# Opening of a four-layer attention kernel: gate loads, input parts and identity products moved

## The chip, the cores and the metric

The kernel runs on one core of a Trainium2 chip. The metric is the device time of one execution in microseconds (us). Five engines run side by side, each through its own list of instructions in order: PE (matrix products; loading of its weights is shown as PEld), DVE (vector), ACT (activations), POOL (GpSimd) and SP, which here only issues DMAs.

## The reference

The input `x` is 2048 tokens of 640 numbers, in float32. Four residual layers follow, A, B, A, B, each on a layer norm of `x`, with 32 heads of 20 numbers. Layers of one kind share their weights.

```python
# A: linear attention
phi = lambda t: jnp.where(t > 0, t + 1, jnp.exp(t)) + 1e-6
pq, pk = phi(q), phi(k)
kv = jnp.einsum("bhsd,bhse->bhde", pk, v)
z  = jnp.einsum("bhsd->bhd", pk)
o  = einsum(pq, kv) / (einsum(pq, z) + 1e-6)          # then @ wo
# B: four segments of 512 tokens; causal softmax inside a segment, a running memory between them
g = _sigmoid(beta).reshape(1, H, 1, 1)
o = g * a_mem + (1.0 - g) * a_dot                     # then @ wo
```

`beta` (32 numbers) is the input that the gate loads below fetch.

## The kernel before

**Tiling.** Tokens go in 4 segments of 512, each in 4 tiles of 128. Products run in fp16 with float32 sums: an operand is kept as an upper part and a lower part (what the upper leaves over), and each product is made of three, upper by upper, upper by lower and lower by upper. For one output bank of 320 columns that is 5 chunks times 3 products (`proj_n`).

**The opening** is the first A layer (`opening`). Besides its own work it prepares all eight weight matrices. `w_prep` does that for one matrix in steps: five loads into a `stage` buffer, five DVE maxima (`wmx`), one maximum over them (`wm1`), a PE transpose of that column (L252), a DVE maximum of the turned row (`wm2`, L254), a PE product with ones that spreads it over the partitions (L258), three DVE instructions to a scale (`inv`, `scl`), then per chunk an ACT write of the upper part (L269) and a DVE write of the lower part (L270), and a store of the result to memory. Between the steps stand `pause`s, which let other work be recorded first. `w_Ak` is prepared at the very start, `A_q` in segment 0, `A_v` and `A_o` in segment 1, then `B_v`, `B_q`, and in segment 3 `B_k` and `B_o`.

In each segment `g_first` makes keys and queries (`phi_a`: ACT exponential and relu, one DVE combination), splits the keys into `pk` (ACT L556 upper, DVE L543 lower), and sums key by input products in `memory` (L580, 12 products a bank, DVE L602 adds them to `G`). Each tile is normalized (`moments`: DVE statistics, a POOL power for `rs`, DVE `nb`; then `normed` on ACT), turned by PE (`turn`: transposes L329, ACT upper L333, DVE lower L334) and also kept unturned as `xs` (`parts`: ACT L487, POOL L488), the weights of the `memory` products. After segment 3, `merge` folds the sums and the weights of `v` and `o` into one matrix: DVE makes `ge` (L661) from `G` and `rz`, ACT and DVE split it into `xT` (L663, L664), PE makes `kt` (L682) and then `wm` (L712, L718). `p_read` prepares query tiles for the next step; its row sum is the DVE reduction L757 into `rca`.

`gates` loads `beta` twice: as `gate` (one DMA) and as `cg` (four DMAs of eight numbers each, into a tile that DVE has filled first, L207). ACT takes exponentials of both (L211, L212), DVE adds one (L213, L214). It is called in `last`, in segment 3.

**What sets the order.** Generators are woven together; the order in which they record is PE's order (PE is scheduled by hand). On the other engines a scheduler places each instruction as early as it thinks it can run. `issue_after(i)` keeps what is recorded in its block behind instruction `i` on the engine of `i`. `busy(n)` records `n` products of the identity with itself, whose result nobody reads; each stands as two entries in the trace.

Of the kernel before, what the change touches and what calls it, by code (L numbers as in the profile page):

```python
# [21 lines left out]
P = 128  # L22
# [6 lines left out]
HN = 320  # L29
# [100 lines left out]
def pause(n):  # L130
    for _ in range(n):
        yield 0.0
# [12 lines left out]
class Kernel:  # L145
# [53 lines left out]
    def gates(self):  # L199


        nc, cp = self.nc, self.cp
        beta = self.A["B_beta"]
        g = cp.tile([P, H], F32, name="gate")
        nc.sync.dma_start(g, bass.AP(tensor=beta.tensor, offset=beta.offset, ap=[[0, P], [1, H]]))
        self.cg = cp.tile([P, NG], F32, name="cg")
        nc.vector.memset(self.cg, -1e4)  # L207
        for h4 in range(4):
            nc.sync.dma_start(self.cg[32 * h4 + DH:32 * h4 + DH + 1],
                              bass.AP(tensor=beta.tensor, offset=beta.offset + h4, ap=[[0, 1], [4, NG]]))  # L210
        nc.scalar.activation(g, g, AF.Exp, scale=-1.0)  # L211
        nc.scalar.activation(self.cg, self.cg, AF.Exp)  # L212
        nc.vector.tensor_scalar(g, g, 1.0, None, op0=OP.add)  # L213
        nc.vector.tensor_scalar(self.cg, self.cg, 1.0, 2.0 ** 100, op0=OP.add, op1=OP.min)  # L214
        self.ginv = g
# [15 lines left out]
    def w_prep(self, key, stage, w, wait=0, behind=None):  # L231


        nc, cp = self.nc, self.cp
        st = stage.tile([P, C, D], F32, tag="stage", name="stage", bufs=2)
        src = self.w_src(key).rearrange("(c p) n -> p c n", p=P)
        mx = cp.tile([P, C], F32, name="wmx", tag="wmx", bufs=2)
        for c in range(C):
            nc.sync.dma_start(st[:, c], src[:, c])
        yield from pause(wait)  # L240
        with self.tc.issue_after(behind.ins) if behind else nullcontext():
            for c in range(C):
# [5 lines left out]
        nc.vector.tensor_reduce(m1, mx, axis=AX.X, op=OP.max)  # L248
        yield 0.0
        yield from pause(wait - 4 if key == ("B", "o") else wait)  # L250
        pt = self.bank()
        nc.tensor.transpose(pt[:1, :P], m1, self.ident)  # L252
        m2 = cp.tile([1, 1], F32, name="wm2", tag="wm2", bufs=2)
        self.last = nc.vector.tensor_reduce(m2, pt[:1, :P], axis=AX.X, op=OP.max)  # L254
        yield 100.0
        yield from pause(wait + 2 if key == ("A", "v") else wait)
        pb = self.bank()
        nc.tensor.matmul(pb[:, :1], self.ones, m2, start=True, stop=True)  # L258
        inv = cp.tile([P, 1], F32, name="inv_%s%s" % key)
        scl = cp.tile([P, 1], F32, name="scl_%s%s" % key)  # L260
        nc.vector.tensor_scalar(inv.bitcast(I32), pb[:, :1].bitcast(I32), 0x7F800000, None,
                                op0=OP.bitwise_and)
        nc.vector.tensor_scalar(inv, inv, 2.0 ** -14, 2.0 ** -114, op0=OP.mult, op1=OP.max)
        self.last = nc.vector.reciprocal(scl, inv)
        self.inv[key], self.scl[key] = inv, scl
        yield 100.0
        for cols in (slice(0, HN), slice(HN, D)) if key == ("A", "k") else (slice(0, D),):
            for c in range(C):
                nc.scalar.activation(w[:, c, 0, cols], st[:, c, cols], AF.Copy, scale=scl)  # L269
                self.last = nc.vector.scalar_tensor_tensor(w[:, c, 1, cols], st[:, c, cols], scl, w[:, c, 0, cols],  # L270
                                                           op0=OP.mult, op1=OP.subtract)
# [50 lines left out]
    def turn(self, src, dst, i):  # L322

        nc = self.nc
        for c0, c1 in ((0, 3), (3, 5)):
            pt = self.bank()
            n = c1 - c0
            for c in range(c0, c1):
                nc.tensor.transpose(pt[:, (c - c0) * P:(c - c0 + 1) * P], src[:, c * P:(c + 1) * P],  # L329
                                    self.ident)  # L330
            v = pt[:, :n * P].rearrange("p (c t) -> p c t", c=n)
            hi = dst[:, c0:c1, 0, i * P:(i + 1) * P]
            nc.scalar.activation(hi, v, AF.Copy)  # L333
            self.lower = nc.vector.tensor_tensor(dst[:, c0:c1, 1, i * P:(i + 1) * P], v, hi, op=OP.subtract)  # L334
            yield n * 110.0

# [3 lines left out]
        self.nc.sync.dma_start(x, src[r:r + P])  # L340
        return x

    def moments(self, x):
# [8 lines left out]
        self.taken = nc.vector.tensor_scalar(rs, mv[:, 1:2], 1e-5, None, op0=OP.add)  # L352
        self.power = nc.gpsimd.tensor_tensor(rs, rs, self.mhalf, op=OP.pow)
        nb = sb.tile([P, 1], F32, tag="nb", name="nb", bufs=4)
        self.last = nc.vector.tensor_scalar(nb, mv[:, 0:1], rs, -1.0, op0=OP.mult, op1=OP.mult)
        return x, nb, rs

    def gather(self, x, mv):
# [36 lines left out]
                yield 9 * SEG * COL  # L395
        return p

    def proj_n(self, xT, w, i, n, p=None, cs=range(C)):

        nc = self.nc  # L400
        if p is None:
            p = self.bank()[:, :HN]
        k = 3 * cs[0]
        for c in cs:
            for a, b in ((0, 0), (0, 1), (1, 0)):
                nc.tensor.matmul(p, xT[:, c, a, i * P:(i + 1) * P], w[:, c, b, n * HN:(n + 1) * HN],  # L406
                                 start=k == 0, stop=k == 3 * C - 1)
                k += 1
        return p

    COST_N = 15 * HN * COL
# [122 lines left out]
    def g_first(self, s, box, w, L, behind=None):  # L534
# [12 lines left out]
        def keys(i):  # L547
# [4 lines left out]
            nc.gpsimd.memset(pk[i][:, 1, HN:HN + 1], 0.0)  # L552
            for n in range(2):
                z, c = slice(n * HN, (n + 1) * HN), slice(n * (HN + 1), n * (HN + 1) + HN)
                e = self.phi_a(self.proj_n(xT, w("k"), i, n), self.inv["A", "k"])
                nc.scalar.activation(pk[i][:, 0, c], e, AF.Copy, scale=self.k_scl)  # L556
                if L["early"] and s == 0 and i < NT - 1:
                    late.append((pk[i][:, 1, c], e, pk[i][:, 0, c]))
# [67 lines left out]
    def merge(self, L, wv, wo, memory, fill):  # L626
# [24 lines left out]
        for n in range(2):  # L651
# [4 lines left out]
            for c in range(C):  # L656
# [7 lines left out]
                nc.vector.tensor_tensor(t[:, c, 1, :HN], e, t[:, c, 0, :HN], op=OP.subtract)  # L664
        L["zb"] = zb
        L["pre"] = [self.p_load(L, 0, i) for i in range(3)]
        for _ in memory:
# [79 lines left out]
    def p_read(self, L, s, i, o, pq=None):  # L747
# [9 lines left out]
        nc.vector.tensor_reduce(rc, q3, axis=AX.X, op=OP.add)  # L757
# [377 lines left out]
    def opening(self, src, stage, L, box):  # L1135
# [15 lines left out]
        def w(n):  # L1151
            for _ in a(n):
                pass
            return self.w["A", n]

        def late():
            self.setup_late(stage)
            yield 0.0

        def last():  # L1160
            self.scales("B")
            with self.tc.issue_after(self.keyed.ins):
                self.gates()
            yield 0.0

        self.lower = self.keyed = self.first = None
        cur = [None, self.x_t(), self.xs_t(0)]
        k = a("k")
# [17 lines left out]
        self.key_scale()  # L1186
        m = [m]
        with self.tc.issue_after(self.last.ins):
# [15 lines left out]
        o = others()  # L1204
        self.ones_columns()
# [160 lines left out]
```

## Time and profile before

| | |
|---|---|
| time, median of 3 executions | 1705.25 us (1703.31 to 1706.91) |
| the profiled execution | 1704.55 us, of which its span is 1702.8 us |
| PE busy | 1637.9 us, 96% of the span, 13788 products |
| DVE busy | 1272.3 us, 75% |
| ACT busy | 994.2 us, 58% |
| POOL busy | 505.9 us, 30% |
| mean granted PE clock | 0.992 of full |
| first A layer | the first 262 us, of which the change touches most |

A row of the timeline gives the start in us, the duration, the engine, the line, the operation, output and inputs by name, the shape and the count; in brackets stands the idle time of the engine ahead of it and what ended that. A row of the windows gives a stretch, its length, busy time (number of instructions), the granted PE clock as a share of full speed, and the use of DMA.

### The profile page before, as it was taken

To read this page: it belongs to the slowest core of one execution; us is meant where nothing else is said; L and a number is where in the kernel's file an instruction comes from. 1 tells how busy PE (TensorE), PEld (TensorE's weight loads), DVE (VectorE), ACT (ScalarE), POOL (GpSimd) and SP (SyncE) were. 2 spreads that over 40 slices of the span, in tenths; PEclk is the share of its full clock that TensorE was granted. 3 is DMA by queue.
4 is the path that set the end of the run, shared out by engine and by line. 5 is a ranking of instruction groups with operands and counts; after the bars stand their busy time and mean duration, and the time that the engine had idled before them with its cause. 6 is when DMAs were issued, how large, how long until landed. Compare 5 with 4: busy or idle time off the path is not lost.

```text
span 1702.8 us, 37843 instructions
## 1 busy us (share of the span) xinstructions
PE 1637.9 (96%) x13788; PEld 1018.6 (60%) x13788; DVE 1272.3 (75%) x4015; ACT 994.2 (58%) x1888; POOL 505.9 (30%) x1046
## 2 busy tenths in 40 slices
PE   7999979999999999999999999999999999999998
PEld 5767757554465556556566777765546545645555
DVE  7888887487887788759874465847888978878773
ACT  6666533347756746667776454333675676666673
POOL 3442222013223322333452210310322332233452
PEclk9999989999999999999999999999999999999999
DMA  6424654421322331353211303423232323323432
GB/s 218 151 75 169 223 203 152 136 98 59 111 79 69 115 118 56 128 183 95 72 56 39 117 32 125 178 94 123 70 110 89 114 83 110 102 86 111 140 103 95
DMA packets 110372, 191.00 MB, mean 112 GB/s; under 512 B 14172, under 2 KB 69596, under 8 KB 107624
## 3 DMA queue, kind: packets, MB, share of 16 engines
q1 hardware_dynamic: 97704, 142.68, 25.9%
q0 software_dynamic: 3264, 24.91, 4.1%
q10 hardware_dynamic: 9216, 20.98, 3.2%
q8 instruction: 109, 1.79, 0.4%
q14 instruction: 79, 0.65, 0.1%
HBM read 109.32 MB, written 78.64 MB: 110 GB/s over the span
## 4 chain that ended last, share of the span: by engine, by line
PE 66%; DVE 17%; ACT 9%; issue 3%; DMA 3%; POOL 2%; SPq 0%; ACTq 0%; POOLq 0%; DVEq 0%
PE ps L406 25%; PE ps L391 13%; PE ps L1061 8%; PE ps L580 4%; PE ps L1034 4%; ACT pe L1038 3%; PE ps L993 3%; PE ps L329 3%; DVE ps L999 3%; PE ps L457 2%; PE ps L1074 1%; DVE e L421 1%; DVE wmx L243 1%; DVE split L270 1%; DVE xT L334 1%
## 5 line engine op out<-in xcount | busy, mean ns | idle before, releaser
L999 DVE CUSTOM_DVE_ANT_0 ps<-ps,maskw 128x512 f32<-128x512 f32 (+3 forms) x1024 | 472.0, 518 | 28.7 <-PE ps L993 25.9
L1038 ACT ACTIVATE pe<-ps,lsc 128x512 f32<-128x512 f32 x640 | 395.4, 696 | 63.0 <-PE ps L1034 59.8
L406 PEld LDWEIGHTS <-xT 128*128 128x128 f16 x2880 | 282.2, 99 | 115.0 <-issue 6.2
L1045 POOL TENSOR_SCALAR_AFFINE_SELECT pe<-pe 128x256 f32<-128x256 f32 (+1 forms) x640 | 233.4, 372 | 350.5 <-ACT pe L1038 342.7
L406 PEld LDWEIGHTS <-oT 128*128 128x128 f16 x1920 | 184.5, 98 | 84.7 <-issue 8.3
L1061 PE MATMUL ps<-pe,v 128*32 128x512 f32 (+3 forms) x2048 | 161.6, 436 | 8.8 <-DVE oT L334 1.9
L406 PE MATMUL ps<-wm,oT 128*128 128x320 f16 x960 | 141.3, 299 | 3.8 <-DVE rs L352 2.6
L406 PE MATMUL ps<-w_Bo,oT 128*128 128x320 f16 x960 | 141.5, 299 | 3.2 <-ACT oT L333 2.0
L406 PE MATMUL ps<-w_Ak,xT 128*128 128x320 f16 x960 | 140.6, 303 | 3.1 <-DVE xT L334 1.0
L406 PE MATMUL ps<-w_Bv,xT 128*128 128x320 f16 x960 | 142.3, 303 | 0.2
L391 PE MATMUL ps<-xT,w_Bq 128*128 128x512 f16 x600 | 140.9, 379 | 1.3 <-ACT pe L1038 0.8
L999 DVE DVE_READ_ACCUMULATOR2_ANT mg<- 128x1 f32 x1024 | 142.1, 139 | 0.1
L580 PE MATMUL ps<-pk,xs 128*128 128x321 f16 (+1 forms) x960 | 140.7, 304 | 1.1 <-DVE pk L543 0.7
L391 PE MATMUL ps<-xT,w_Bk 128*128 128x512 f16 x600 | 138.5, 379 | 1.2 <-ACT pe L1038 1.2
L406 PE MATMUL ps<-w_Aq,xT 128*128 128x320 f16 x960 | 137.6, 299 | 0.1
L993 PE MATMUL ps<-ks,qs 60*128 60x512 f16 (+3 forms) x1024 | 123.5, 297 | 7.6 <-ACT pe L1038 3.5
L580 PEld LDWEIGHTS <-xs 128*128 128x128 f16 x960 | 93.9, 99 | 41.0 <-issue 1.6
L421 DVE SCALAR_TENSOR_TENSOR e<-e,r 128x320 f32<-128x320 f32 x128 | 69.6, 544 | 53.6 <-ACT r L420 53.0
L1034 PE MATMUL ps<-qs,ks 62*128 62x512 f16 (+3 forms) x1024 | 105.6, 300 | 2.1 <-ACT pe L1038 1.1
L1061 PEld LDWEIGHTS ps<-pe,v 128*32 128x32 f32 x2048 | 65.4, 109 | 68.7 <-issue 40.9
L831 DVE SCALAR_TENSOR_TENSOR nat<-ps,nat 128x512 f16<-128x512 f32 x80 | 55.2, 690 | 62.6 <-ACT nat L830 62.3
L391 PEld LDWEIGHTS <-w_Bk 128*128 128x128 f16 x600 | 57.1, 98 | 66.5 <-issue 6.4
(202 smaller groups left out, 2359.6 us busy)
## 6 DMA issues: line engine op xcount, KB each, us to landing
x<-xn ACTq DMA_DIRECT2D x48, 320.0 KB
qs<-qd SPq DMA_DIRECT2D x128, 120.0 KB
ks<-kd SPq DMA_DIRECT2D x128, 120.0 KB
xo<-x SPq DMA_DIRECT2D x48, 320.0 KB
pqi<-pqd SPq DMA_DIRECT2D x32, 320.0 KB
qd<-nat SPq DMA_DIRECT2D x40, 256.0 KB
kd<-nat SPq DMA_DIRECT2D x40, 256.0 KB
x<-in_A_x SPq DMA_DIRECT2D x16, 320.0 KB
```

What stands on the lines that cost most here:

```text
L329: nc.tensor.transpose(pt[:, (c - c0) * P:(c - c0 + 1) * P], src[:, c * P:(c + 1) * P], self.ident)
L391: nc.tensor.matmul(p, w[:, c, a, t * P:(t + 1) * P], xT[:, c, b, :], start=k == 0, stop=k == 3 * C - 1)
L406: nc.tensor.matmul(p, xT[:, c, a, i * P:(i + 1) * P], w[:, c, b, n * HN:(n + 1) * HN], start=k == 0, stop=k == 3 * C - 1)
L421: nc.vector.scalar_tensor_tensor(e, e, 1.0, r, op0=OP.min, op1=OP.add)
L580: nc.tensor.matmul(p, xs[:, i, a, c * P:(c + 1) * P], pk[i][:, b, cols], start=i == 0 and a == b, stop=i == NT - 1 and a == 1)
L831: nc.vector.scalar_tensor_tensor(nat[:, 1], p, QK_SHIFT, nat[:, 0], op0=OP.mult, op1=OP.subtract)
L993: nc.tensor.matmul(bs[par][:, a:a + n], qs[r, p, i * P:(i + 1) * P], ks[r, p, :n], start=True, stop=True)
L999: nc.vector.tensor_tensor_reduce(bs[par][:, a:a + n], bs[par][:, a:a + n], self.maskw[:, SEG - n:], 1.0, NEG, OP.add, OP.max, G["mg"][:, p ...
L1034: nc.tensor.matmul(b[:, a:a + n], ks[r, p, j * P:(j + 1) * P], qs[r, p, j * P:], start=True, stop=True)
L1038: nc.scalar.activation(e, b, AF.Exp, scale=self.lsc)
L1045: nc.gpsimd.affine_select(d, d, pattern=pat, compare_op=OP.is_ge, fill=0.0, base=0, channel_multiplier=-1)
L1061: nc.tensor.matmul(G["pv"][32 * h4:32 * h4 + 32, j * P:], v[j][:, h * E1:h * E1 + 32], G.pop((p, par, j)), start=j == 0, stop=j == 2, skip ...
```

## The change

1. `gates` is split by a `yield`. Its loads are recorded in segment 1 (`late`, at the step `next(gates)`), the exponentials and additions in segment 3 as before, now behind the ACT instruction that last wrote an upper part of a turned tile (`self.upper`).
2. In segment 0 `parts` of a tile is recorded after the turn of the next tile and behind its ACT write and the last power on POOL, instead of all four after the last turn.
3. `busy`: 11 instead of 5 after the first turn, the 3 before `A_k`'s ones product instead of behind it, 5 behind it, and 4 after the second key product. With `cold`, the first key bank takes lower by upper ahead of upper by lower.
4. `moments` can stop ahead of `nb`; for tile 1 `nb` (`shift`) comes later among the lower parts of `w_Ak`.
5. `A_v` pauses 8 steps instead of 2 ahead of its ones product.
6. `p_read`'s row sum goes behind the last lower part that `merge` wrote (`L["parted"]`).

```diff
+        yield 0.0
+        with self.tc.issue_after(self.upper.ins):
+            nc.scalar.activation(g, g, AF.Exp, scale=-1.0)
+            nc.scalar.activation(self.cg, self.cg, AF.Exp)
...
-        yield from pause(wait + 2 if key == ("A", "v") else wait)
+        yield from pause(wait + 8 if key == ("A", "v") else wait)
...
+            for a, b in ((0, 0), (1, 0), (0, 1)) if cold else ((0, 0), (0, 1), (1, 0)):
...
+                if cold and k == 2 and n == 0:
+                    self.busy(4)
...
+        with self.tc.issue_after(L["parted"].ins):
+            nc.vector.tensor_reduce(rc, q3, axis=AX.X, op=OP.add)
...
         def late():
             self.setup_late(stage)
+            next(gates)
             yield 0.0
...
             with self.tc.issue_after(self.keyed.ins):
-                self.gates()
+                next(gates, None)
...
-        self.busy(5)
+        self.busy(11)
         with self.tc.high_priority():
-            for _ in range(4):
+            for _ in range(3):
                 next(k)
             self.busy(3)
+            next(k)
+            self.busy(5)
             with self.tc.issue_after(self.last.ins):
-                m = self.moments(x[1])
+                m = self.moments(x[1], False)
             with self.tc.issue_after(self.taken.ins):
-                w("k")
+                for _ in range(5):
+                    next(k)
+            with self.tc.issue_after(self.last.ins):
+                m = self.shift(*m)
+            w("k")
...
-            with self.tc.issue_after((self.keyed or top).ins):
-                for i in range(NT):
-                    self.parts(xh[i], cur[2], i)
+                for j in range(i - 1, NT if i == NT - 1 else i):
+                    with self.tc.issue_after(self.upper.ins), self.tc.issue_after(top.ins):
+                        self.parts(xh[j], cur[2], j)
```

How instructions stand on the engines, before and in the change (in these rows a line of the changed file is 2 to 7 higher for the same instruction). First DVE at the end of segment 3, where `wm_2790` and `wm_2815` are the turned maximum of `B_o`. Before:

```order
L570 TENSOR_SCALAR e<-e 128x320
L602 TENSOR_TENSOR v_81<-ps,v_81 128x321
L659 TENSOR_SCALAR eps<-v_81,k_scl 128x1
L214 TENSOR_SCALAR cg<-cg 128x8
L602 TENSOR_TENSOR v_82<-ps,v_82 128x321
L254 TENSOR_REDUCE wm_2790<-ps 1x1
```

In the change, the same place:

```order
L577 TENSOR_SCALAR e<-e 128x320
L609 TENSOR_TENSOR v_81<-ps,v_81 128x321
L666 TENSOR_SCALAR eps<-v_81,k_scl 128x1
L609 TENSOR_TENSOR v_82<-ps,v_82 128x321
L256 TENSOR_REDUCE wm_2815<-ps 1x1
```

The addition on `cg` has moved up beside that on `gate`, seven rows earlier. The filling of `cg` now stands fourth on DVE in the whole program, its four DMAs stand on SP right behind that of `gate` and ahead of the store of `w_Ak`, and both exponentials stand on ACT in segment 2, behind a turned tile.

Then PE at the start of the program, from the end of the first turn to the first key products. Before:

```order
L320 MATMUL ps<-ident 128x128 x5
L252 MATMUL ps<-ident,wm_163 1x128
L258 MATMUL ps<-wm_167,ones 128x1
L320 MATMUL ps<-ident 128x128 x3
L406 LDWEIGHTS xT
L406 MATMUL ps<-w_Ak,xT 128x320
```

In the change:

```order
L322 MATMUL ps<-ident 128x128 x11
L254 MATMUL ps<-ident,wm_169 1x128
L322 MATMUL ps<-ident 128x128 x3
L260 MATMUL ps<-wm_173,ones 128x1
L322 MATMUL ps<-ident 128x128 x5
L411 LDWEIGHTS xT
L411 MATMUL ps<-w_Ak,xT 128x320
L411 LDWEIGHTS xT
L411 MATMUL ps<-w_Ak,xT 128x320
L322 MATMUL ps<-ident 128x128 x4
```

Fifteen identity products are new, and three have gone ahead of the ones product. On DVE, `nb` of tile 1 stood behind the first of the ten lower parts of `w_Ak` and stands behind the sixth; on ACT and POOL the `xs` work has left the place ahead of the second key bank's exponential and ahead of the powers.

Last, PE between segments 1 and 2, where `wm_1574`/`wm_1633` is the column of `A_o` and `wm_1606`/`wm_1651` its turned maximum. Before:

```order
L580 LDWEIGHTS xs
L580 MATMUL ps<-pk,xs 128x320
L258 MATMUL ps<-wm_1606,ones 128x1
L406 LDWEIGHTS xT
L406 MATMUL ps<-w_Ak,xT 128x320
```

In the change:

```order
L587 LDWEIGHTS xs
L587 MATMUL ps<-pk,xs 128x320
L254 MATMUL ps<-ident,wm_1633 1x128
L260 MATMUL ps<-wm_1651,ones 128x1
L411 LDWEIGHTS xT
L411 MATMUL ps<-w_Ak,xT 128x320
```

The transpose of `A_o` stood 24 memory products ahead of its ones product and now stands right before it. `A_v`'s ones product stood ahead of the first memory product of segment 1 and now stands behind the 36th. On DVE the scale of `A_v` and its first lower parts go behind three of the copies L602, and the casts of the constants (L187, L188) behind the lower parts of `A_o`.

More of the change, by code (lines that the diff above doesn't have):

```diff
@@ L332, in turn @@
             hi = dst[:, c0:c1, 0, i * P:(i + 1) * P]
-            nc.scalar.activation(hi, v, AF.Copy)
+            self.upper = nc.scalar.activation(hi, v, AF.Copy)
             self.lower = nc.vector.tensor_tensor(dst[:, c0:c1, 1, i * P:(i + 1) * P], v, hi, op=OP.subtract)
@@ L341, in load_x, with moments @@
         return x
-    def moments(self, x):
+    def moments(self, x, whole=True):
         nc, sb = self.nc, self.sb
@@ L353, in moments, with shift @@
         self.power = nc.gpsimd.tensor_tensor(rs, rs, self.mhalf, op=OP.pow)
-        nb = sb.tile([P, 1], F32, tag="nb", name="nb", bufs=4)
-        self.last = nc.vector.tensor_scalar(nb, mv[:, 0:1], rs, -1.0, op0=OP.mult, op1=OP.mult)
+        return self.shift(x, mv, rs) if whole else (x, mv, rs)
+    def shift(self, x, mv, rs):
+        nb = self.sb.tile([P, 1], F32, tag="nb", name="nb", bufs=4)
+        self.last = self.nc.vector.tensor_scalar(nb, mv[:, 0:1], rs, -1.0, op0=OP.mult, op1=OP.mult)
         return x, nb, rs
@@ L396, in proj_t, with proj_n @@
         return p
-    def proj_n(self, xT, w, i, n, p=None, cs=range(C)):
+    def proj_n(self, xT, w, i, n, p=None, cs=range(C), cold=False):
         nc = self.nc
@@ L404, in proj_n @@
         for c in cs:
-            for a, b in ((0, 0), (0, 1), (1, 0)):
+            for a, b in ((0, 0), (1, 0), (0, 1)) if cold else ((0, 0), (0, 1), (1, 0)):
                 nc.tensor.matmul(p, xT[:, c, a, i * P:(i + 1) * P], w[:, c, b, n * HN:(n + 1) * HN],
@@ L554, in keys @@
                 z, c = slice(n * HN, (n + 1) * HN), slice(n * (HN + 1), n * (HN + 1) + HN)
-                e = self.phi_a(self.proj_n(xT, w("k"), i, n), self.inv["A", "k"])
+                e = self.phi_a(self.proj_n(xT, w("k"), i, n, cold=L["early"] and s == 0 and i == 0), self.inv["A", "k"])
                 nc.scalar.activation(pk[i][:, 0, c], e, AF.Copy, scale=self.k_scl)
@@ L663, in merge @@
                 nc.scalar.activation(t[:, c, 0, :HN], e, AF.Copy)
[L664 removed]
+                L["parted"] = nc.vector.tensor_tensor(t[:, c, 1, :HN], e, t[:, c, 0, :HN], op=OP.subtract)
         L["zb"] = zb
@@ L1162, in last @@
             with self.tc.issue_after(self.keyed.ins):
-                self.gates()
+                next(gates, None)
             yield 0.0
+        gates = self.gates()
         self.lower = self.keyed = self.first = None
```

3 lines of the change are left out of this document (removed).

## The prediction

> **What bounds the kernel now.** The page first: PE is busy 96% of the span, so only its idle time and its clock can give anything, and nearly all the change touches the first 262 us. There I asked who waited for whom on PE.
>
> ```profile
> PE ps L258 <- DVE wm L254: 8.1, 3, 5.6
> ```
>
> The columns are total us, times and the longest. One wait of 5.6 us stands out: a ones product waits for a turned maximum. The timeline shows why:
>
> ```profile
> 218.39 0.21 DVE L659 TENSOR_SCALAR eps<-v,k_scl 128x1 f32<-128x1 f32 x1
> 223.50 0.21 ACT L212 ACTIVATE cg<-cg 128x8 f32<-128x8 f32 x1 [6.59 <-DMA cg<-in_B_beta]
> 223.75 0.17 DVE L214 TENSOR_SCALAR cg<-cg 128x8 f32<-128x8 f32 x1 [5.14 <-ACT cg L212]
> 223.82 0.48 DVE L602 TENSOR_TENSOR v<-ps,v 128x321 f32<-128x321 f32 x1
> 224.64 0.55 PE L258 MATMUL ps<-wm,ones 1*128 1x1 f32 x2 [5.61 <-DVE wm L254]
> 216.06 2.87 SPq L209 DMA_DIRECT2D cg<-in_B_beta  x4
> 218.30 5.10 DMA cg<-in_B_beta
> ```
>
> `B_o`'s maximum is queued on DVE behind the addition on `cg`, that behind ACT's exponential, that behind four small DMAs issued only at 216.06; the last row, from the chain of waits, is the flight of the last one. PE's clock is the second thing. The windows of PE, cut where the granted clock changed (every 3.41 us):
>
> ```profile
> 10.02:13.43 3.41, 1.61 (x10) 1.00 1.04 407
> 13.43:16.85 3.41, 2.54 (x10) 0.50 0.53 192
> 16.85:20.26 3.41, 3.41 (x14) 0.50 0.14 60
> 20.26:23.67 3.41, 2.26 (x16) 1.00 0.98 360
> 109.01:112.42 3.41, 1.62 (x12) 1.00 0.13 48
> 112.42:115.83 3.41, 3.30 (x13) 0.50 0.13 48
> 245.54:248.95 3.41, 1.23 (x12) 1.00 0.57 160
> 248.95:252.37 3.41, 3.37 (x31) 0.50 0.93 392
> ```
>
> After a window with PE busy for about half or less (1.61, 1.62, 1.23 us) the next runs at half clock; after a full one it is whole again; 2.26 us did not lower it. Where these windows begin in another execution I can't know, so each wait of a few us is a gamble. The profiled execution took 1704.55 us, 0.7 under the median of 1705.25. Sums are made against it; I count 0.2% (3.4 us) as what a measurement can tell from no change.
>
> **Term 1, the opening: -0.8 us.**
>
> ```profile
> 8.19 1.28 PE L320 MATMUL ps<-ident 128*128 128x128 f32 x10
> 10.75 0.27 PE L252 MATMUL ps<-ident,wm 128*1 128x128 f32 x1 [1.28 <-DVE wm L248]
> 11.73 0.38 PE L258 MATMUL ps<-wm,ones 1*128 1x1 f32 x2 [0.71 <-DVE wm L254]
> 15.54 5.99 PE L406 MATMUL ps<-w_Ak,xT 128*128 128x320 f16 x26 [0.17 <-DVE w_Ak L270]
> 14.82 0.21 DVE L355 TENSOR_SCALAR nb<-mv,rs 128x1 f32<-128x1 f32 x1 [0.45 <-POOL rs L353]
> 14.95 4.24 DVE L270 SCALAR_TENSOR_TENSOR w_Ak<-stage,scl_Ak,w_Ak 128x320 f16<-128x320 f32 x9
> 20.76 0.14 DVE L352 TENSOR_SCALAR rs<-mv 128x1 f32<-128x1 f32 x1
> 21.13 1.43 POOL L488 TENSOR_TENSOR xs<-xh,xs 128x640 f16<-128x640 f32 x1 [6.26 <-ACT xs L487]
> 22.52 0.54 POOL L353 TENSOR_TENSOR rs<-rs,mhalf 128x1 f32<-128x1 f32 x1
> 23.10 0.21 DVE L355 TENSOR_SCALAR nb<-mv,rs 128x1 f32<-128x1 f32 x1 [1.80 <-POOL rs L353]
> 23.80 0.54 DVE L334 TENSOR_TENSOR xT<-ps,xT 128x384 f16<-128x384 f32 x1
> 24.40 0.45 PE L406 MATMUL ps<-w_Ak,xT 128*128 128x320 f16 x2 [1.00 <-DVE xT L334]
> 40.41 0.30 PE L580 MATMUL ps<-pk,xs 128*128 128x321 f16 x1 [0.22 <-ACT pk L556]
> 41.17 0.84 PE L580 MATMUL ps<-pk,xs 128*128 128x321 f16 x5 [0.47 <-DVE pk L543]
> ```
>
> The identity products (1.28 us for five before) sit in PE's waits ahead of the transpose and of the ones product (1.28 and 0.71 us) and among the first key products, and should keep the window from 10.02 full, so the first 30 key products run at full clock and end with DVE's last lower part. That is 0.4 us earlier, since DVE no longer waits 0.45 us for `nb` among them: 18.8 instead of 19.19, and PE ends at 19.2 instead of 21.53. This by itself brings nothing, since PE then waits for the next tile. What ends that wait is a queue: `xs` (1.43 us) stands on POOL ahead of the power, DVE's `nb` waits 1.80 us for it, and the turned tile's lower part stands behind `nb`. With `xs` moved behind, the power runs right after `rs`, at 20.5 instead of 22.52; one bank's combination, ready later, takes back some 0.2. The lower part comes at 22.0, and PE resumes at 22.6 instead of 24.40: **-1.8**. What is late next is the clock: the turn ends near 19.7, ACT's upper part lets two products go near 20.6, and the rest waits till 22.5, so PE is idle for some 2.4 of 2.8 us, less busy than the windows that fell above. I expect one window at half clock, which costs 3.41/2 = 1.7. Of that, 0.7 is covered, because PE waits 0.22 and 0.47 near 41 for `pk`, from a DVE chain that has come 1.8 earlier too. So -1.8 + 1.7 - 0.7 = -0.8; ends -1.8 (clock holds) and 0 (falls for longer).
>
> **Term 2, `A_v` behind 36 products: +1.9 us.**
>
> ```profile
> 112.01 0.35 PE L258 MATMUL ps<-wm,ones 1*128 1x1 f32 x2 [1.79 <-DVE wm L254]
> 112.29 3.91 PE L580 MATMUL ps<-pk,xs 128*128 128x321 f16 x14
> 112.89 2.24 DVE L543 SCALAR_TENSOR_TENSOR pk<-e,k_scl,pk 128x320 f16<-128x320 f32 x1 [0.63 <-ACT pk L556]
> ```
>
> The wait of 1.79 us goes, but it hides another: the memory products need the last tile's `pk`, which DVE finishes at 112.89 + 2.24 = 115.13, and nothing ahead of it on DVE or ACT depends on the ones product. PE now starts products at 110.2, does the ten that need no lower `pk` in 1.4 us, and stands still from 111.6 to 115.2. No gain, and 3.6 us of idle in one piece lowers the clock: one to two windows at half speed in busy time, 1.6 to 3.3 us, where before the low window fell on the ten products that had to wait anyway and cost 0.3 (115.2 to 115.83 at half). Middle +1.9, ends 0 and +3.0.
>
> **Term 3, `A_o`'s transpose next to its ones product: +0.9 us.**
>
> ```profile
> 127.25 0.27 PE L252 MATMUL ps<-ident,wm 128*1 128x128 f32 x1
> 130.73 0.38 PE L258 MATMUL ps<-wm,ones 1*128 1x1 f32 x2
> ```
>
> Where the two stand together, as at 10.75 in the opening, the second starts 0.98 us after the first, and PE's queue (all keys of segment 2) waits behind it. At 127.25 there were 24 products between. 0.98 less 0.1 of issue is 0.9; ends 0.5 (DVE free at once) and 1.2 (DVE's last copy, 0.48, just ahead).
>
> **Term 4, the end of segment 3: -6.1 us.** Both exponentials now run in segment 2 on data fetched in the first 20 us; the L602 at 223.82 can follow `eps` at 218.47: -5.35. PE then comes to its products 5.3 earlier, and they end earlier still at full clock, but DVE's run (reciprocals, `ge`, `w_Bo`) is what is late next:
>
> ```profile
> 240.26 1.99 PE L682 MATMUL ps<-xT,w_Av 128*128 128x140 f16 x30
> 247.34 0.80 DVE L757 TENSOR_REDUCE rca<-pqi 128x32 f32<-128x640 f32 x1
> 248.06 0.87 DVE L664 TENSOR_TENSOR xT<-ge,xT 128x320 f16<-128x320 f32 x2
> 248.59 4.06 PE L682 MATMUL ps<-xT,w_Av 128*128 128x80 f16 x35 [0.89 <-DVE xT L664]
> ```
>
> It works without a break until 248.9 and ends PE's last wait there (0.89 us). So PE gets DVE's -5.35, and the row sum taken out ahead of L664 gives another 0.7: -6.1 at 248.59. The 35 products behind took 4.06 us at half clock; at the 1.99/30 of the row at 240.26 they would take 2.3, so 1.7 more if the clock holds. PE waits longer there than before (it comes earlier to a DVE that moved less), so I don't count on it. Ends -5.35 and -7.8.
>
> **At nothing.** The gate DMAs hold SP 2.87 us near 11 us, where SP's next, the store of `w_Ak`, has to wait for the last lower part (19.19) anyway. Fifteen more identity products take some 0.25 us each (1.28 for five), 3.8 in all, and lie in waits of term 1; what of them sticks out, some 0.1 at each of four places, ends in the wait for DVE's lower parts. The casts of the constants and `B_v`'s load move past `A_o`'s lower parts at a place where the waits view has PE waiting for neither; late by the 4 to 6 us of those lower parts, the load still has the ten or more until `B_v`'s maxima. Ends 0 and +0.5. The second merge runs under attention's products, which give PE other work; ends -0.3 and +0.3.
>
> Sum: -0.8 + 1.9 + 0.9 - 6.1 = -4.1, so 1700.4.
>
> **The page on the clock.** The Trainium skill ("TensorE: Matmul & The Clock Gate", Part 1, "What's actually happening") says that the clock halves after at least one idle window of about 3.4 us and doubles after a busy one, the windows running free. The length agrees (3.41); but the rows above show falls after windows that were 1.2 to 1.6 us busy, so here a wholly idle window isn't needed, and the measurement decides. By the page's rule the waits of terms 1 and 2 would seldom hold a whole window, which is the first rival.
>
> **Rivals.**
> - *The clock holds at every new wait* (gate falls only after an empty window). Term 1 -1.8, term 2 -0.3, term 3 +0.9, term 4 -7.8: -9.0, **1695.6**. For: 2.26 us of 3.41 didn't lower it. Against: the three falls. Chance 0.22.
> - *The clock falls for two windows at each.* Term 1 0, term 2 +3.0, term 3 +1.2, term 4 -5.35: -1.2, **1703.4**, no change to a measurement. For: 13.43 to 20.26 was two windows. Chance 0.14.
> - *`A_o`'s maximum takes the place of the old wait.* DVE's run for `A_v` (five lower parts and the copies, 118.2 to 126.3 before, 8.1 us) now starts some 3 us later, and the turned maximum stands behind it with all of PE behind that. It decides once the run ends after PE's products, about 3 us later still; if all of it stood there, +8.1: **1708.5**, 4.0 over the profiled execution and so slower. Against: 3 us of slack. Chance 0.04.
> - *The wait stays,* the loads or exponentials holding up something else instead: +5.3, **1705.7**. Against: 130 us between load and use. Chance 0.02.
>
> **The numbers.** The forecast has 0.58, by itself 1698 to 1702.5; about a sixth of that, 0.10, lies above 1701.1, where faster by 3.4 than 1704.55 ends. Faster: 0.48 + 0.22 = 0.70; same: 0.10 + 0.14 + 0.02 = 0.26; slower: 0.04. The range takes in the first rival's value and the second's; the third lies outside.
>
> **What would show it.** Right: no `cg` wait near 215 and the ones product within 0.5 us of its products; PE resuming at 22 to 23 in the opening; a PE idle of about 3.6 us ahead of L587 near 113, low clock behind it; 0.9 us between the two `A_o` products. Wrong: PE not waiting for `pk` in segment 1, the clock full throughout, or a new wait for `wm` near 130 or 219.

## The result, and the profile after

The change takes 1697.61 us (median of 9 executions, 1695.49 to 1702.47) against 1704.97 us (9 executions, 1703.29 to 1709.40) of the kernel before on the same chip. The ratio is 0.9961, with a 95% interval of 0.9953 to 0.9969: 5 to 8 us faster. Run again later, beside other kernels, it gave 1697.55 us and a ratio of 0.9955 (0.9941 to 0.9969). The forecast of 1700.4 was 2.8 us too high: inside its range, which takes in two of its rivals, but 0.4 below the 1698 to 1702.5 that it gave to its own mechanism.

The profiled execution of the change happens to be the slowest of its nine: 1702.47 us, span 1700.8. So the two traces are compared place by place. A shift below is the start of the same PE instruction in the change less its start before; a line of the changed file is 2 to 7 higher. In PE's waits in the first 262 us (total us, times, longest), the old first row (8.1 us for `wm`) has shrunk to 1.0, and the largest wait for `wm` is 0.7:

```profile
PE ps L689 <- DVE xT L671: 2.5, 6, 0.6
PE ps L587 <- DVE pk L550: 2.4, 2, 2.0
PE ps L260 <- DVE wm L256: 1.0, 2, 0.7
```

What took its place is the wait for `pk` and for the parts of `ge` (`xT` L671). PE's timeline of the change, at the places of the four terms:

```profile
22.77 3.55 PE L411 MATMUL ps<-w_Ak,xT 128*128 128x320 f16 x13 [1.64 <-DVE xT L336]
40.99 0.38 PE L260 MATMUL ps<-wm,ones 1*128 1x1 f32 x2
111.09 0.31 PE L587 MATMUL ps<-pk,xs 128*128 128x321 f16 x1 [0.68 <-ACT pk L563]
113.36 2.91 PE L587 MATMUL ps<-pk,xs 128*128 128x321 f16 x20 [1.96 <-DVE pk L550]
128.82 0.27 PE L254 MATMUL ps<-ident,wm 128*1 128x128 f32 x1
129.75 0.38 PE L260 MATMUL ps<-wm,ones 1*128 1x1 f32 x2 [0.66 <-DVE wm L256]
213.25 0.31 PE L587 MATMUL ps<-pk,xs 128*128 128x321 f16 x1 [0.51 <-ACT pk L563]
214.00 2.09 PE L587 MATMUL ps<-pk,xs 128*128 128x321 f16 x14 [0.45 <-DVE pk L550]
219.24 0.35 PE L260 MATMUL ps<-wm,ones 1*128 1x1 f32 x2 [0.31 <-DVE wm L256]
248.50 0.99 PE L725 MATMUL ps<-w_Ak,kt 128*32 128x320 f16 x6
```

and, of before, the rows that answer to them and that the prediction doesn't show:

```profile
41.95 0.38 PE L258 MATMUL ps<-wm,ones 1*128 1x1 f32 x2
214.11 2.09 PE L580 MATMUL ps<-pk,xs 128*128 128x321 f16 x14 [0.26 <-DVE pk L543]
253.39 0.99 PE L718 MATMUL ps<-w_Ak,kt 128*32 128x320 f16 x6
```

From these starts: -1.63 where PE resumes in the opening, -0.96 near 41, -0.98 at `A_o`'s ones product (130.73 before), -0.11 at 214, -5.40 at `B_o`'s ones product (224.64 before), **-4.89** behind the merge. In segment 1, where PE resumes with the last `pk`, the products that were grouped with the row at 112.29 started at 115.19 and start at 113.36: -1.83. So the first A layer gives -4.89 in this pair; its terms are -0.96, -0.87, +0.85, +0.87 (new, near 213) and -4.78. One pair is not the kernel: the change was profiled a second time, at 1697.55 us, and there PE is ahead by 0.65 near 41, 1.26 at the last `pk`, 0.41 at `A_o`'s ones product, 0.64 at 214 and 6.16 behind the merge.

The windows of PE in the change, cut where the granted clock could change (columns: stretch, length, busy time, clock, DMA):

```profile
19.49:22.91 3.42, 1.18 (x8) 1.00 1.12 419
22.91:26.32 3.41, 3.41 (x14) 0.50 0.73 250
108.24:111.65 3.41, 2.48 (x17) 1.00 0.26 95
111.65:115.07 3.42, 1.71 (x13) 1.00 0.01 2
241.36:244.77 3.41, 1.88 (x25) 1.00 0.63 193
244.77:248.19 3.42, 3.42 (x28) 0.50 0.94 387
1637.41:1640.82 3.41, 2.46 (x21) 1.00 0.87 292
1640.82:1644.23 3.41, 2.70 (x11) 0.50 0.02 5
```

The opening now runs at full clock to 22.91, where it ran at half from 13.43 to 20.26 before; one half window follows, as forecast. In segment 1 the clock holds. The last fall, at 1640.82, lasts two windows, lies in code that the change doesn't touch and was not there before; it goes with this execution being the slowest of its nine. Over the first nine executions of the change the mean granted clock is 0.9971; over 29 of the kernel before it is 0.9935. That is 2 x 0.0029 x 1696 = 9.8 us at half clock against 2 x 0.0065 x 1703 = 22.1 us, 12.3 us less, worth at most half of that, since part of it fell into waits. Among those 29 executions of one kernel a mean clock higher by 0.001 goes with 1.2 us less time; by that, as an estimate, the difference of 0.0036 is 4.2 of the 7.4 us. So a good part of the gain is clock. In the trace of before, four of its eight half-clock windows lie at two places that the change mends: 13.43 to 20.26, and 221.65 to 228.47 at the `cg` wait and behind it.

### The profile page after: what moved, and what is told of

It reads as the page before. It is cut to its first block, busy times and chain, and to the rows that moved or that the text cites. A ratio compares the mean times of both kernels' runs of the same rounds, so it can differ in the third digit from the quotient of the medians.

```text
span 1700.8 us, 37903 instructions
## 1 busy us (share of the span) xinstructions
PE 1638.9 (96%) x13818; PEld 1020.3 (60%) x13818; DVE 1268.7 (75%) x4015; ACT 994.6 (58%) x1888; POOL 506.4 (30%) x1046
## 4 chain that ended last, share of the span: by engine, by line
PE 70%; DVE 15%; ACT 8%; issue 3%; DMA 2%; POOL 1%; SPq 1%; ACTq 0%; POOLq 0%; DVEq 0%
PE ps L411 28%; PE ps L396 13%; PE ps L1069 8%; PE ps L587 5%; PE ps L1042 4%; ACT pe L1046 4%; PE ps L1001 3%; PE ps L331 3%; DVE ps L1007 2%; PE ps L464 2%; PE ps L1082 1%; DVE e L428 1%; DVE wmx L245 1%; DVE st L350 1%; DVE xT L336 1%
## 5 line engine op out<-in xcount | busy, mean ns | idle before, releaser
L587 PE MATMUL ps<-pk,xs 128*128 128x321 f16 (+1 forms) x960 | 137.6, 300 | 3.6 <-DVE pk L550 2.4
L587 PEld LDWEIGHTS <-xs 128*128 128x128 f16 x960 | 92.7, 97 | 41.6 <-DVE pk L550 2.8
```

Of the source, the lines that this page charges most:

```text
L587: nc.tensor.matmul(p, xs[:, i, a, c * P:(c + 1) * P], pk[i][:, b, cols], start=i == 0 and a == b, stop=i == NT - 1 and a == 1)
```

## The experiments

All times are medians, and each ratio, with its 95% interval in brackets, is to the kernel before on the same chip (1704.82 to 1706.26 us).

**Gates alone** (edit 1 in the kernel before).

```diff
...
+        yield 0.0
+        with self.tc.issue_after(self.upper.ins):
+            nc.scalar.activation(g, g, AF.Exp, scale=-1.0)
+            nc.scalar.activation(self.cg, self.cg, AF.Exp)
...
```

> The kernel before with edit 1 alone (gate loads in segment 1, exponentials behind a turned tile). Theory: the 5.35 us that DVE stood behind the addition on cg go, but DVE then reaches its two ge instructions (1.29 us before) while POOL multiplies the third query tile by z, because that tile's transfer lands late, so they take some 2.3 us and about 1.0 comes back: 4.4 us faster than before, and the pair of ge in the trace 2.2 to 2.3 us. Rival A (the forecast's step): 5.3 us faster, ge 1.3 us. Rival B: the moved loads and exponentials hold up other work, gain under 3 us.

Measured: 1700.78 us, ratio 0.9977 (0.9967 to 0.9988), 4.1 us faster. DVE's and POOL's timelines at the place in question:

```profile
228.44 1.32 DVE L663 SCALAR_TENSOR_TENSOR ge<-v,eps,rz 128x320 f32<-128x320 f32 x2
224.24 4.71 POOL L756 TENSOR_TENSOR pqi<-pqi,z 128x640 f32<-128x640 f32 x3 [2.56 <-DVE z L648]
```

The transfer was in time here: POOL's three multiplications run without a break beside DVE's reciprocals, and the pair of `ge` takes 1.32 us. So my expectation that `ge` is stretched whenever the `cg` wait goes was wrong; it hangs on when the third tile lands (the run with earlier loads, below, shows it). That leaves rival A, 5.3 us. The interval (2.0 to 5.6 us) can't part it from the 4.4 of my theory; the trace bears it out from segment 3 on, while the median fell short of it:

```profile
219.69 1.81 PE L582 MATMUL ps<-pk,xs 128*128 128x321 f16 x12
250.82 0.99 PE L720 MATMUL ps<-w_Ak,kt 128*32 128x320 f16 x6
```

The same two groups stand at 217.23 and 253.39 before: +2.46 when it enters the end of segment 3, -2.57 when it leaves, so 5.03 gained there. The 2.46 were lost earlier: up to there this execution ran at half clock for four windows against three before, and in two of the four (from 25.23 and from 117.39) PE was busy throughout.

**The opening alone** (edits 2, 3, 4), and then with the block of edit 1 that keeps the exponentials back, the loads staying in segment 3:

```diff
...
+        with self.tc.issue_after(self.upper.ins):
+            nc.scalar.activation(g, g, AF.Exp, scale=-1.0)
+            nc.scalar.activation(self.cg, self.cg, AF.Exp)
...
```

> The kernel before with edits 2, 3 and 4 alone (xs behind the next turn, identity products, nb later). Theory: PE is 0.8 to 1.0 us earlier at the first memory products near 40 us, and DVE's run in segment 1 loses some 0.8 us more of sharing with POOL (the xs products meet other instructions), so that the wait of segment 1 ends 1.8 us earlier: 1.8 us faster. Rival A (the forecast's term 1): what is gained is what PE has at 41 us, 0.8 us faster. Rival B: nothing, because the wait in segment 1 takes it all back, 0.

> The kernel before with edits 2, 3 and 4 and, of edit 1, only the block that keeps both exponentials behind a turned tile's upper part; the loads stay in segment 3. Theory: the 4 us that the opening alone lost are ACT standing at the gate exponential ahead of the parts of w_Ak until its load lands; with the block ACT starts those parts at 13.0 us, PE is 0.9 to 1.0 us earlier at 41 us and 1.8 us earlier behind the wait of segment 1, the cg wait of 5.6 us stays: 1 to 2 us faster than before. Rival: the opening edits lose by themselves (their own queues), and the time stays 1 to 2 us above before.

Measured: alone 1706.90 us, ratio 1.0017 (1.0007 to 1.0026), **slower** by 2.0; with the block 1702.80 us, ratio 0.999 (0.998 to 1.0), 2.0 faster, with an interval that just reaches no change. ACT and PE in the opening alone:

```profile
16.88 0.23 ACT L211 ACTIVATE gate<-gate 128x32 f32<-128x32 f32 x1 [7.33 <-DMA gate<-in_B_beta]
17.61 0.69 PE L409 MATMUL ps<-w_Ak,xT 128*128 128x320 f16 x2 [3.73 <-ACT w_Ak L269]
```

and ACT with the block:

```profile
13.26 4.63 ACT L270 ACTIVATE w_Ak<-stage,scl_Ak 128x320 f16<-128x320 f32 x10 [4.08 <-DVE scl_Ak L265]
```

The scheduler had put the gate's exponential ahead of the ten upper parts of `w_Ak`, where it waits for a load whose issue is at 10.96, and all of ACT with it: 3.7 us. Before, the same instruction stood at 32.4 us, where its data had long come. So the block in edit 1 is not only part of the gates' move; the opening edits lose without it. What I had written as their theory before the first of these runs (-1.8) fits only with it. Edits 2 and 4 and the order of the products in edit 3 were not run apart: that the opening's gain comes from `xs` standing behind the power is read from the rows, not tested.

**`A_v`'s ones product back ahead of the memory products** (edit 5 undone).

```diff
-        yield from pause(wait + 8 if key == ("A", "v") else wait)
+        yield from pause(wait + 2 if key == ("A", "v") else wait)
```

> The change with edit 5 undone (A_v's ones product ahead of the memory products again). Theory: that ones product only stood in front of another wait that ends at the same place, and the edit's one lasting effect is A_o's transpose next to its ones product (0.85 us): 0.9 us faster than the change, 0.3 less if the clock falls near 113 as it did before. Rival A (the forecast's terms 2 and 3): 2.8 us faster than the change. Rival B (the pause is worth what it was made for): 1 us or more slower than the change.

Measured: 1699.40 us, ratio 0.9974 (0.9963 to 0.9984); the change has 0.9961 (0.9953 to 0.9969). So it is not 2.8 us faster, which refutes the forecast's price, and my own theory (0.9 faster) missed too; by the medians rival B is nearest, but 1.8 us slower lies at the edge of what the intervals part. PE's timeline, and below it its windows:

```profile
113.94 12.35 PE L587 MATMUL ps<-pk,xs 128*128 128x321 f16 x86 [0.35 <-DVE pk L550]
129.60 0.38 PE L260 MATMUL ps<-wm,ones 1*128 1x1 f32 x2
```

```profile
108.01:111.42 3.41, 1.48 (x12) 1.00 0.13 48
111.42:114.84 3.42, 3.06 (x13) 0.50 0.16 53
```

Here the clock falls, PE resumes with `pk` 0.6 us later than in the change (113.94 against 113.36), and wins it back at `A_o`, whose ones product comes at 129.60 against 129.75. In this pair of executions edit 5 and its price at `A_o` cancel, so the traces don't show where 1.8 us would come from.

**`A_o` earlier and six identity products more.** The transpose three steps earlier, and `busy(6)` behind tile 1's turn.

```diff
-        yield from pause(wait - 4 if key == ("B", "o") else wait)
+        yield from pause(wait - 4 if key == ("B", "o") else 0 if key == ("A", "o") else wait)
...
                 if i == 1:
+                    self.busy(6)
                     yield 0.0
```

> The change with two additions: A_o's transpose three steps earlier (twelve products ahead of its ones product), and six identity products behind the turn of tile 1, to keep PE busy from 20.1 to 21.6 us. Theory: the 0.66 us wait of A_o's ones product goes and with it 0.85 us; the window from 22.9 to 26.3 us stays at full clock, which gives 1.0 us at the first memory products near 41 us, of which the wait for pk in segment 1 may take all: 0.9 to 1.9 us faster than the change. Rival: the clock is lowered in that window all the same and A_o's maximum still waits: no gain.

Measured: 1697.68 us, ratio 0.9962 (0.9948 to 0.9977), the time of the change. Both steps did what they were to do in the trace (`A_o`'s ones product without a wait, PE at full clock behind tile 1), and no gain can be measured in the time. In the trace PE takes its lead through segment 1's wait for `pk`, which is as long as in the change and ends 1.5 us sooner (113.36 there):

```profile
111.84 3.73 PE L587 MATMUL ps<-pk,xs 128*128 128x321 f16 x26 [1.96 <-DVE pk L550]
```

Behind the merge this execution is 7.02 us ahead of that of before, where the change's two have 4.89 and 6.16. Why the median shows none of it was not settled.

**Without the fifteen added identity products,** run twice.

```diff
-        self.busy(11)
+        self.busy(5)
...
             next(k)
-            self.busy(5)
...
-                if cold and k == 2 and n == 0:
-                    self.busy(4)
```

> The change without its fifteen added identity products (5 after the first turn, none behind the ones product or the second key product). Theory: the clock falls near 13 us as it did before, the first 30 key products run at half clock and end near 21.5 us, which the wait for tile 1's lower part (until 22.8 us) mostly hides; one more half-clock window, 0 to 1 us slower than the change. Rival A: the products at half clock delay the first key combinations, and with them z and the powers on POOL, and PE resumes 1.5 us later or more: 1.5 to 3 us slower. Rival B: the added products cost PE time, and without them it is 0.5 us faster.

> The change without its fifteen added identity products, once more. Theory from its first runs: the added products only move the half-clock window from 13 us to 23 us, so the times agree within 1 us with the change. Rival: without them 1.3 us or more faster, as the four first runs had it.

Measured: 1696.32 us (0.9951, 0.9937 to 0.9965) and 1696.71 us (0.9951, 0.9937 to 0.9965), beside 1697.55 us (0.9955) of the change on the same chip as the second:

> The change itself, once more, beside the next two on one chip: 6 to 8 us faster than before, as first measured.

The identity products bring nothing that can be measured in the time. The windows without them:

```profile
9.44:12.86 3.42, 1.37 (x10) 1.00 1.04 408
12.86:16.27 3.41, 2.29 (x9) 0.50 0.73 265
19.68:23.10 3.42, 2.39 (x17) 1.00 1.10 419
```

The first key products run at half clock, as before the change, but PE then ends them later, idles less in the next window (2.39 us busy instead of 1.18), and keeps full clock behind it. So here the added products moved the low clock from 13 to 23 us, from products that had to wait for DVE anyway to products that hadn't. This is not fixed: of the three executions profiled without them, this one ran at half clock for two windows on end (12.86 to 19.68), the second for one, the third (the second combination below) for two apart.

Read with the clock, the runs say more. Over 14 executions of the change the mean clock is 0.9971 and the mean time 1698.1 us; over the nine without the added products they are 0.9961 and 1696.7. So the products do keep the clock up and the time is no shorter for it: they seem to cost elsewhere what the clock gives. The traces agree. PE's shift against the trace of before, in us:

| | near 41 | at the last `pk` of segment 1 | at 214 | behind the merge |
|---|---|---|---|---|
| the change | -0.96 | -1.83 | -0.11 | -4.89 |
| the change, second trace | -0.65 | -1.26 | -0.64 | -6.16 |
| without the fifteen | -1.65 | -3.20 | -2.78 | -10.16 |
| the same, second trace | -1.33 | -2.87 | -2.44 | -8.59 |

Near 41 us both traces without them are ahead of both with them, and the lead grows. The times of these few runs can't confirm it.

**Edit 6 undone** (executed once).

```diff
-        with self.tc.issue_after(L["parted"].ins):
-            nc.vector.tensor_reduce(rc, q3, axis=AX.X, op=OP.add)
+        nc.vector.tensor_reduce(rc, q3, axis=AX.X, op=OP.add)
```

> The change with edit 6 undone (p_read's row sum free to go ahead of the last lower part of ge). Theory: the row sum of 0.8 us stands ahead of the last lower part again and PE's last products of the first bank come 0.6 to 0.7 us later (shift at the products L689 near 244 us). Rival: the row sum fits into idle time of DVE there and the shift is under 0.2 us.

DVE's timeline:

```profile
239.83 1.28 DVE L671 TENSOR_TENSOR xT<-ge,xT 128x320 f16<-128x320 f32 x3
241.96 0.80 DVE L764 TENSOR_REDUCE rca<-pqi 128x32 f32<-128x640 f32 x1
242.69 0.87 DVE L671 TENSOR_TENSOR xT<-ge,xT 128x320 f16<-128x320 f32 x2
```

The sum stands ahead of the last lower parts again. In the change the three lower parts start at 240.77 and the last two at 243.04, so DVE's lead of 0.94 us has become 0.35: 0.59 us lost, as the theory had it (0.6 to 0.7) for DVE. On PE the shift can't be read, since its clock fell to half at 241.92. Its one time is 1700.24 us.

**Two combinations.** The first adds to the change `A_o` earlier, `busy(6)`, pairs of identity products in the merge, and the loads of the query tiles ahead of the store of `w_Bk`. The second leaves out all added identity products and keeps `A_o` and the loads.

```diff
...
+        if L["early"]:
+            with self.tc.issue_after(self.staged.ins):
+                L["pre"] = [self.p_load(L, 0, i) for i in range(3)]
...
+                    if t == 2 and n == 1 and c > 0:
+                        spare = self.bank() if c == 1 else spare
+                        for _ in range(2):
+                            nc.tensor.matmul(spare[:, :P], self.ident, self.ident, start=True, stop=True)
...
```

> The change with four additions: A_o's transpose three steps earlier and six identity products behind tile 1's turn (as tried), pairs of identity products among the last products that wait for ge in the merge, and the three loads of query tiles ahead of the store of w_Bk on SP. Theory: the loads land before POOL needs them, POOL multiplies beside DVE's reciprocals, the pair of ge takes 1.3 us instead of 2.26, which brings PE 1.0 us; the identity products keep the clock in the 3.4 us that ran at half near 245 us, up to 1.6 us more: 1.5 to 3.5 us faster than the change. Rival A: ge keeps its 2.2 us (no gain from the loads). Rival B: the identity products delay the last merge products by as much as the clock gives: same time as the change.

> The change without the fifteen identity products, with A_o's transpose three steps earlier and the three loads of query tiles ahead of the store of w_Bk. Theory: 0.85 us from the transpose and 0.9 us from the pair of ge (1.3 us instead of 2.26 or 1.83), no identity products in the second merge: 1.2 to 1.8 us faster than the kernel without identity products. Rival: the earlier products meet pk's lower part in segment 1 or near 213 us and wait there, and the gain is under 0.5 us.

Measured: the first 1701.42 us, ratio 0.9981 (0.9971 to 0.9991), 3.8 us slower than the change; the second 1697.16 us, ratio 0.9948 (0.9931 to 0.9965), the time of the change. DVE and PE of the first, and the window of PE in segment 1:

```profile
226.17 1.30 DVE L671 SCALAR_TENSOR_TENSOR ge<-v,eps,rz 128x320 f32<-128x320 f32 x2
111.46 5.41 PE L587 MATMUL ps<-pk,xs 128*128 128x321 f16 x26 [1.96 <-DVE pk L550]
1073.13 0.69 PE L695 MATMUL ps<-ident 128*128 128x128 f32 x4
```

```profile
108.11:111.52 3.41, 0.84 (x6) 1.00 0.13 48
```

The loads did what they were meant to: all three multiplications run beside the reciprocals (POOL's start at 221.98 and take 4.68 us without a break), and `ge` takes 1.30 us; products that are 0.13 us ahead of the change at its 213.25 are 0.99 ahead at its 234.32, and behind the first merge this execution is 7.47 us ahead of that of before. Two losses stand in the trace. The pairs also went into the second merge, near 1075 us, where PE waits for nothing: eight more products of a quarter of a us, and 2.1 us of shift there. And PE, 2 us early in segment 1, idles so long for `pk` that only 0.84 us of the window are busy; the clock falls, and 26 products take 5.41 us instead of 3.73. That costs the lead and no more: at 118 us PE is 2.35 ahead of before, and 2.12 in the change. So the second merge explains 2.1 of the 3.8 us, and where the rest comes from stays open. The second combination has neither loss, its `ge` takes 1.30 us and `A_o`'s ones product has no wait (128.56 us), and still its time can't be told from that of the kernel without identity products, so my theory of 1.2 to 1.8 us missed. So none of these versions beats the change by what can be measured.

## Why the prediction was right or wrong

The time lies in the range and the sign is right, but that the sum came near is luck. The four terms were forecast at -0.8, +1.9, +0.9 and -6.1; the pair of traces has -0.96, -0.87, +0.85 and -4.78, and +0.87 at a place the forecast didn't name: -4.89 against -4.1. An error of 2.8 us in term 2 and errors of 1.3 and 0.9 us the other way, in term 4 and near 213, nearly cancelled. The medians differ by 7.4: one pair doesn't show it all, and the second trace of the change, with -6.16 behind the merge, has a span 7.0 us shorter than that of before.

- **Term 1 was right in its steps:** PE resumes at 22.77 (forecast 22.6), one half-clock window follows, -0.96 is left near 41 (forecast -0.8). What it did not see is that the added identity products have no part in the gain: it put them "at nothing", and both traces without them are further ahead near 41 us (1.65 and 1.33 against 0.96 and 0.65).
- **Term 2 had the right wait and the wrong sign.** PE does stand for `pk` once the ones product is gone, 0.68 and 1.96 us. The step that failed is the one that put the end of that wait at 115.2 and priced its idle time by the clock. The end came at 113.36, because DVE's run came 1.82 us earlier (L550 at 111.07, 112.89 before), 0.86 more than PE's own lead. DVE's rows say where that came from, before and in the change:

```profile
73.58 1.22 DVE L421 SCALAR_TENSOR_TENSOR e<-e,r 128x320 f32<-128x320 f32 x1 [1.42 <-ACT r L420]
75.84 1.96 DVE L421 SCALAR_TENSOR_TENSOR e<-e,r 128x320 f32<-128x320 f32 x1 [0.69 <-ACT r L420]
78.92 3.07 DVE L570 TENSOR_SCALAR e<-e 128x320 f32<-128x320 f32 x1
```

```profile
73.89 0.49 DVE L428 SCALAR_TENSOR_TENSOR e<-e,r 128x320 f32<-128x320 f32 x1 [1.42 <-ACT r L427]
76.16 0.49 DVE L428 SCALAR_TENSOR_TENSOR e<-e,r 128x320 f32<-128x320 f32 x1 [1.42 <-ACT r L427]
78.83 1.73 DVE L428 SCALAR_TENSOR_TENSOR e<-e,r 128x320 f32<-128x320 f32 x1
```

  Three instructions of 0.3 to 0.5 us were stretched while POOL multiplied `xs`; in the change one is. Two of POOL's multiplications before:

```profile
76.03 1.42 POOL L488 TENSOR_TENSOR xs<-xh,xs 128x640 f16<-128x640 f32 x1
79.04 2.76 POOL L488 TENSOR_TENSOR xs<-xh,xs 128x640 f16<-128x640 f32 x2
```

  And the clock held, after 2.48 and 1.71 us of busy time, as it did in the second trace of the change; where PE came earlier still it did fall (0.84, first combination), so the gamble that the forecast named is real, but it was counted as lost. The forecast's rule was also drawn from too few windows: it says that 2.26 us busy did not lower the clock, and another window of that same trace, with 2.26 us busy too, did (last section).
- **Term 3 was right** (+0.85 against +0.9), and no measurable time hangs on it: with the transpose moved away the time stays.
- **Term 4 was mis-sized:** its step "PE gets DVE's -5.35" left out what DVE runs into. The `cg` wait went (-5.29 from 214 to `B_o`'s ones product) and the row sum gave 0.59, but DVE now reaches `ge` while POOL is late with the third query tile:

```profile
226.22 1.55 POOL L761 TENSOR_TENSOR pqi<-pqi,z 128x640 f32<-128x640 f32 x1 [1.00 <-DMA pqi<-pqd]
226.32 2.26 DVE L668 SCALAR_TENSOR_TENSOR ge<-v,eps,rz 128x320 f32<-128x320 f32 x2
```

  That pair took 1.29 us before and takes 1.30 with the loads issued earlier (1.89 in the second trace of the change); 0.97 us is lost here, which is most of what the term lacks: -5.29 + 0.97 - 0.59 is -4.91, and -4.78 was measured.
- **The +0.87 near 213** is once more a wait for `pk` (0.51 and 0.45 us, 0.26 before): PE came 0.98 early to a DVE that had moved only 0.1. DVE was 1.0 us early too until one of `B_o`'s maxima had to wait for its load:

```profile
202.60 0.82 DVE L245 TENSOR_REDUCE wmx<-stage 128x1 f32<-128x640 f32 x1 [0.82 <-DMA stage<-in_B_wo]
```

  In the second trace of the change that wait is 0.48 us, and PE loses nothing there (0.41 ahead at `A_o`, 0.64 at 214).
- **"At nothing" missed a tie between edits:** the exponentials' new place was counted only as a gain in segment 3, though the opening needs it (4 us between the two opening runs).
- **Rivals:** the clock holding everywhere (1695.6) is nearer to the median than the forecast is; the traces show it holding at term 2 alone. The waits that the two last rivals spoke of did not come.
- **Its own signs:** no `cg` wait near 215, PE resuming at 22.77 and 0.93 us between the two `A_o` products came as it said. The idle time ahead of L587 was 2.64 us (0.68 and 1.96) instead of 3.6, with no low clock behind it, and a small new wait for `wm`, 0.31 us, stands at 219, which it had among the signs of being wrong.

The Trainium skill bears on both stretched places ("SBUF — State Buffer", "Who interferes with whom"): a DVE instruction with two inputs in SBUF contends with a POOL instruction that reads SBUF, and the second to start is blocked. The rows agree on who contends: `ge` and `e<-e,r` (two SBUF inputs) go from about 0.5 us to between 1.22 and 1.96 beside POOL, while `v<-ps,v`, with one input in PSUM, keeps 0.42 to 0.48 beside the same multiplications. They leave two things open. `e<-e` (L570), with one input, is stretched most, from 0.33 to 3.07. And who was second doesn't always show: the instructions at 75.84 and 78.92 are recorded 0.19 and 0.12 us ahead of POOL's multiplications and still end behind them.

## What to carry to other kernels

When a wait of several us goes, follow the freed engine to its next instructions and look what the other engines and transfers do at that new hour: here, in one trace, a transfer 1 us late cost 1 us of the 5.3. A guard that only seems to belong to one edit may hold the order for another, so run the edits apart and not only together. Filling idle time to keep the clock pays only if what runs at full clock afterwards is not waiting anyway, and fillers must not reach a second call of the same code where nothing waits.

## What the runs showed of the hardware that was not expected

- **The busy share of a window does not decide the clock alone.** Windows with 1.71 and 1.45 us of 3.41 busy (the change at 111.65, and the run with six more identity products at 109.84, whose row is below) were followed by full clock; windows with 1.88 and 2.46 us busy were followed by half clock. One trace, that of before, has both with the same figure: 2.26 us busy from 20.26, then full clock, and 2.26 from 1197.86 (below), then half until 1204.68. What else decides was not settled. The length agrees with the Trainium skill's 3.4 us ("TensorE: Matmul & The Clock Gate", Part 1, "What's actually happening"); a wholly idle window was not needed at any of these falls.

```profile
1197.86:1201.27 3.41, 2.26 (x17) 1.00 0.21 82
109.84:113.25 3.41, 1.45 (x12) 1.00 0.09 33
113.25:116.66 3.41, 3.41 (x26) 1.00 0.13 48
```

- **The time of one and the same kernel follows the number of such windows:** the change took 1695.49 us at a mean clock of 0.999 and 1702.47 at 0.994, and over its nine executions 0.001 of clock goes with 1.4 us. An edit worth under 2 us has to be read from paired instructions too, not from the times alone, and from more than one trace: behind the merge the two traces of the change stand 1.3 us apart.
